# Attention's state products in 64x64 quarters of TensorE, and a mixture-of-experts opening taken by thirds of its tokens

## The chip, the cores and the metric

The kernel runs on one core of a Trainium2 chip. The metric is device time in microseconds (us) of one execution. All times compared here are of runs in the fast state (none is more than 1.5% above the fastest run of the same kernel); no slow run occurred. Beside the times, every run has a span (from its first to its last instruction) and a mean granted TensorE clock (1.00 is full speed), and each kernel has one profiled execution, from which all positions within the span are read. The span is 1.7 us or so shorter than the time of the same run.

## The reference

The program is a linear attention with a decaying state, then a mixture of eight experts with a balanced, greedy assignment. Everything is float32. Cut to what matters:

```python
B, H, S, D = 4, 8, 768, 48                   # r, k, v of this shape; decay w and bonus u per head and channel
for t in range(S):                           # attention
    kt, vt, rt = k[:, :, t], v[:, :, t], r[:, :, t]
    cur = einsum('bhd,bhe->bhde', u * kt, vt)
    y[:, :, t] = einsum('bhd,bhde->bhe', rt, state + cur)
    state = w[:, :, None] * state + einsum('bhd,bhe->bhde', kt, vt)
x = y.transpose(0, 2, 1, 3).reshape(3072, 384)
logits = x @ w_gate                          # 8 experts, 384 tokens each, taken in order of the logit
...
for e in range(8):
    mask = assigned == e
    out[mask] = relu(x[mask] @ w1[e]) @ w2[e]     # w1 384x1024, w2 1024x384
```

## The kernel before

Attention works in 24 units (4 batches x 6 chunks of 128 tokens; 8 heads, in 4 pairs). In each, TensorE transposes r and k, multiplies r with the state of the chunks before (`from_state`), forms the pair products inside the chunk (`pairs`), adds the outputs to the same bank of PSUM, the memory that holds TensorE's results (`outputs`) and forms the new state. The 8 heads' states lie in two row groups; every product from the state uses all 128 rows, half of which are zeros, and 64 columns:

```python
    y_pss, g_pss = ([ps.tile([128, HP, T], F32, ...) for i in range(2)] for name in "yg")   # two banks each
    def from_state(n):
        y_ps = y_pss[n % 2]
        if c > 0:
            for a in range(HP):
                for q in range(2):
                    nc.tensor.matmul(y_ps[halves[q], a, :], state[b][:, a, q, :], live[n]["rT"][:, a, :], start=(a == 0), ...)
    def outputs(n):
        ...                                                  # 8 products onto the same y_ps
        nc.scalar.copy(turned[n], y_ps)
        if c < C - 1:
            ...                                              # 8 products for the new state, kv_ps
            for q in range(2):
                nc.vector.tensor_add(own, own, kv_ps[heads[q]])      # 48 partitions
                nc.gpsimd.tensor_mul(own, own, wc)
    ...
            for n in range(N):                               # order on TensorE of one unit
                mild.rows_turned(n + 2); mild.keys_turned(n + 2); ...
                from_state(n)
                pairs(n + 1)
                outputs(n)
```

The experts come after that. For each expert a search on the logits, interleaved with the products of the expert before, yields a list of tokens; GpSimd fetches their rows from memory by an indirect transfer; TensorE transposes them (`turn`), multiplies with w1 (`hidden`, 8 columns of 128) and with w2 (`result`, 3 row groups of 8 products).

```python
    awake = ...
    for _ in range(7):                                       # keeps TensorE busy until the rows land
        nc.tensor.matmul(awake, ident, LG...)
    walk.settle(ahead, ask(number, w1), fetch(xg))           # rows by GpSimd, the whole of w1 by SyncE
    xT = turn(xg, ahead)
    for n in range(E):
        walk.behind = hidden(hid, 0, at["w1"], xT)
        ahead = following(...)                               # search for the next expert's tokens
        for j in range(1, KF):
            hidden(hid, j, at["w1"], xT)
        for c in range(NC):
            if c == NC - 1 and n + 1 < E:
                xT = turn(ahead["xg"])                       # next expert's transposes, one row group early
            result(n, c, hid, at["w2"], at["tok"])
```

## Time and profile before

The time before is 429.79 us (median of 3 runs, 428.57 to 432.33). The timeline of TensorE cuts the profiled span of 426.7 us into four parts. The first "list" is the small product that ends the search for the first expert's tokens, and the third part ends where the second expert's hidden products begin.

| part of the span, from TensorE's timeline | before, us |
|---|---|
| start to the first pair products | 13.91 |
| first pair products to the first list (140.06) | 126.15 |
| first list to the second expert's hidden products (187.86) | 47.80 |
| the rest | 238.84 |

The lines of attention, of VectorE beside it and of the gap before the first expert are in the prediction below. One stretch that it only tells is worth seeing, TensorE's timeline before around the second expert's list. The columns are start, duration, engine (PE is TensorE, DVE VectorE, ACT ScalarE, POOL GpSimd), line, operation, result and operands, shapes, number of records (a float32 product leaves two, a transpose one), and, in brackets, how long the engine idled before and what ended that.

```profile
170.88 0.18 PE L1133 MATMUL list_ps<-part,alike 128*128 128x12 f16 x1
170.92 10.95 PE L1267 MATMUL o_ps<-w,hid 128*128 128x384 f32 x32
181.71 0.82 PE L1249 MATMUL xT_ps<-ident,xg 128*128 128x128 f32 x6
```

Sixteen output products (32 records) lie between the list and the first transposes that need the listed rows. The rows land behind them, and there is no bracket: TensorE does not wait.

### The profile page before, as it was taken

The page shows a single profiled execution, that of the slowest core. Times are in us where ns is not written, and L with a number is a line of the kernel's source. Part 1 is how long each engine was busy: PE and PEld are TensorE (multiplying, and loading weights), DVE is VectorE, ACT ScalarE, POOL GpSimd, SP SyncE. Part 2 cuts the span into 40 slices and gives each one's busy share as a digit, 9 for nine tenths or more (in the row PEclk, how much of TensorE's full clock was granted, in tenths as well). Part 3 has the DMA queues.
Part 4 walks back from the last instruction along what each step waited for, and adds up shares of the span by engine and source line. Part 5 has one row for each costly group of instructions (what it writes and reads, how often), then busy time and mean ns, then how long its engine had stood idle before and what let it go on. Part 6 is the DMA issues. An engine that isn't in the chain of part 4 may idle for free. (4 is left out here: it accounts for less than half of the span.)

```text
span 426.7 us, 7898 instructions
## 1 busy us (share of the span) xinstructions
PE 405.7 (95%) x2926; PEld 271.6 (64%) x2926; DVE 206.6 (48%) x676; ACT 153.3 (36%) x390; POOL 122.0 (29%) x170
## 2 busy tenths in 40 slices
PE   6999999999998589999999999999999999999993
PEld 3788888888877345565565565565555555566551
DVE  5999889898758247218307506605703702000000
ACT  4888877777747022022122122122121211212200
POOL 5655866676300200310310310210130041211011
PEclk9999999999999699999999999999999999999999
DMA  9999999530018661910910830550460496201001
GB/s 145 170 174 183 168 185 154 116 73 2 3 57 313 205 231 47 324 38 7 336 47 18 260 129 21 193 197 18 152 238 18 144 325 217 75 18 37 2 18 37
DMA packets 93560, 54.38 MB, mean 127 GB/s; under 512 B 76736, under 2 KB 88128, under 8 KB 93504
## 3 DMA queue, kind: packets, MB, share of 16 engines
q1 hardware_dynamic: 89248, 42.49, 40.1%
q0 software_dynamic: 3072, 9.44, 6.2%
q10 hardware_dynamic: 1184, 1.77, 1.4%
q8 instruction: 27, 0.44, 0.5%
q14 instruction: 29, 0.24, 0.2%
HBM read 44.25 MB, written 9.44 MB: 126 GB/s over the span
## 5 line engine op out<-in xcount | busy, mean ns | idle before, releaser
L1260 PE MATMUL h_ps<-xT,w 128*128 128x384 f32 x384 | 133.3, 496 | 0.6 <-ACT xT L1250 0.6
L1267 PE MATMUL o_ps<-w,hid 128*128 128x384 f32 x384 | 129.4, 489 | 0.9
L1267 PEld LDWEIGHTS o_ps<-w,hid 128*128 128x128 f32 x384 | 71.1, 191 | 48.3 <-issue 4.4
L1260 PEld LDWEIGHTS h_ps<-xT,w 128*128 128x128 f32 x384 | 69.0, 191 | 41.8 <-issue 4.9
L1261 ACT ACTIVATE hid<-h_ps 128x384 f32<-128x384 f32 x64 | 31.4, 490 | 101.3 <-PE h_ps L1260 89.8
L1190 POOL DMA_INDIRECT xg<-x_rows,tok x24 | 23.5, 979 | 149.3 <-issue 106.7
L453 ACT ACTIVATE AT<-ident,dd 128x128 f32<-128x128 f32 x192 | 58.9, 394 | 2.0 <-DVE dd L448 2.0
L1270 POOL DMA_INDIRECT out_dram<-o_sb,tok x24 | 23.6, 982 | 113.9 <-ACT o_sb L1269 113.9
L1269 ACT COPY o_sb<-o_ps 128x384 f32<-128x384 f32 x24 | 11.5, 478 | 111.4 <-PE o_ps L1267 106.7
L847 DVE TENSOR_TENSOR own<-counts,same 128x64 f32<-128x64 f32 x21 | 4.7, 225 | 83.5 <-PE counts L859 83.5
L516 DVE COPY_PREDICATED AT<-mask,g_ps 128x512 f32<-128x512 uint8 x48 | 32.6, 732 | 8.6 <-PE g_ps L514 8.3
L514 PE MATMUL g_ps<-rT,kT 48*128 48x128 f32 x384 | 28.4, 285 | 0.2
L445 POOL TENSOR_TENSOR rk<-rk,u_bc 128x384 f32<-128x384 f32 x24 | 27.5, 1145 | 1.9
L444 POOL TENSOR_TENSOR rk<-rt,kt 128x384 f32<-128x384 f32 x24 | 24.2, 1007 | 9.3 <-DMA rt<-in_r_dram 4.4
L514 PEld LDWEIGHTS g_ps<-rT,kT 48*128 48x128 f32 x384 | 23.6, 187 | 4.3 <-issue 1.9
L535 PE MATMUL y_ps<-AT,vt 128*64 128x128 f32 x384 | 26.2, 279 | 0.0
L535 PEld LDWEIGHTS y_ps<-AT,vt 128*64 128x64 f32 x384 | 20.5, 137 | 2.8
L549 POOL TENSOR_TENSOR state<-state,wp 48x192 f32<-48x192 f32 x32 | 16.1, 502 | 20.5 <-DVE state L548 19.3
L524 PE MATMUL y_ps<-rT,state 128*64 128x128 f32 x320 | 21.8, 279 | 0.0
L434 DVE TENSOR_TENSOR ks<-kt,wk 128x384 f32<-128x384 f32 x24 | 20.4, 850 | 0.0
L524 PEld LDWEIGHTS y_ps<-rT,state 128*64 128x64 f32 x320 | 17.1, 137 | 3.1 <-issue 2.7
L473 ACT COPY kT<-kT_ps 128x512 f32<-128x512 f32 x24 | 14.0, 584 | 13.6 <-PE kT_ps L471 13.6
(189 smaller groups left out, 403.1 us busy)
## 6 DMA issues: line engine op xcount, KB each, us to landing
w<-in_moe_w_dram SPq DMA_DIRECT2D x15, 1536.0 KB, 8.3
kt<-in_k_dram SPq DMA_DIRECT2D x24, 192.0 KB, 4.2
rt<-in_r_dram SPq DMA_DIRECT2D x24, 192.0 KB, 4.2
vt<-in_v_dram SPq DMA_DIRECT2D x24, 192.0 KB, 4.9
x_rows<-AT SPq DMA_DIRECT2D x8, 192.0 KB, 2.7
w<-in_moe_w_dram ACTq DMA_DIRECT2D x1, 1536.0 KB
x_rows<-rt SPq DMA_DIRECT2D x6, 192.0 KB, 1.9
x_rows<-ks SPq DMA_DIRECT2D x5, 192.0 KB, 3.0
```

What stands on the lines that cost most here:

```text
L444: nc.gpsimd.tensor_mul(rk, rt[:, :, 0:D], kt)
L445: nc.gpsimd.tensor_mul(rk, rk, self.u_bc.rearrange("p (h d) -> p h d", h=H))
L453: self.tc.nc.scalar.activation(AT[:, h % 2, h // 2, :], self.ident, AF.Copy, scale=dd[:, h:h + 1])
L514: nc.tensor.matmul(g_pss[q][:, a, :], kT[heads[q], a, :], rT[heads[q], a, :], start=True, stop=True)
L516: nc.vector.copy_predicated(out=AT[:, q], mask=mask.unsqueeze(1).to_broadcast([128, HP, T]), data=g_pss[q])
L524: nc.tensor.matmul(y_ps[halves[q], a, :], state[b][:, a, q, :], live[n]["rT"][:, a, :], start=(a == 0), stop=False, skip_group_check=True)
L535: nc.tensor.matmul(y_ps[halves[q], a, :], vt[:, 2 * a + q, :], AT[:, q, a, :], start=(c == 0 and a == 0), stop=(a == HP - 1), skip_group_c ...
L1190: nc.gpsimd.indirect_dma_start(out=xg[:, c, :], out_offset=None, in_=x_dram, in_offset=bass.IndirectOffsetOnAxis(ap=tok[:, c:c + 1], axis=0))
L1260: product = nc.tensor.matmul(h_ps, w1[:, f, ts(j, 128)], xT[:, f, :], start=(f == 0), stop=(f == KD - 1))
L1261: nc.scalar.activation(hid[:, j, :], h_ps, AF.Relu)
L1267: nc.tensor.matmul(o_ps, hid[:, j, ts(c, 128)], w2[:, j, :], start=(j == 0), stop=(j == KF - 1))
L1270: nc.gpsimd.indirect_dma_start(out=out_rows[n * NC + c], out_offset=bass.IndirectOffsetOnAxis(ap=tok[:, c:c + 1], axis=0), in_=o_sb, in_of ...
```

## The change

It has two halves, which share no instruction.

*Attention.* The state is kept in four quarters, so that a product from it uses 48 rows and 64 columns and four such products are meant to lie side by side in the array. The rest follows from this: x gets one set of two PSUM banks instead of two sets of one, the next unit's pair products come ahead of the products from the state so that ScalarE has time to copy x out, both state additions become one over 128 partitions, and one product of 512 columns clears the state's bank at the start.

*First expert.* Half of w1 is asked for as soon as the expert is known, four filler products are to keep TensorE's clock up while the branch is left, and the first four of the eight columns of hidden products are opened by thirds: as soon as 128 of the 384 tokens are transposed, products with them begin.

```diff
+    y_ps = ps.tile([128, 2, HP, T], F32, name="y_ps")
+    order = [(g, j, i) for g in range(2) for j in range(2) for i in range(2)]
     def from_state(n):
         if c > 0:
+            for g, j, i in order:
+                a = 2 * g + i
+                nc.tensor.matmul(y_ps[halves[i], j, g, :], state[b][heads[j], a, :],
+                                 live[n]["rT"][heads[j], a, :], start=(g == 0), stop=False, skip_group_check=True)
-            for a in range(HP):
-                for q in range(2):
-                    nc.tensor.matmul(y_ps[halves[q], a, :], state[b][:, a, q, :], live[n]["rT"][:, a, :], ...
 ... (new_state: one addition and one scaling over 128 partitions)
+            nc.tensor.matmul(kv_ps, state[0][:, 0:2, :].rearrange("p a d -> p (a d)"),
+                             ident.unsqueeze(1).to_broadcast([128, HP, T]), start=True, stop=True)
 ... (the loop over units)
-                from_state(n)
                 if n + 1 < N:
                     pairs(n + 1)
+                from_state(n)
+                new_state(n)
                 outputs(n)
 ... (leaving the attention branch)
+        def between(most):
+            rows(most or N)
+            if not most:
+                for _ in range(4):
+                    nc.tensor.matmul(g_pss[0][:, 0:3, :], ident, ...)
 ... (first expert)
+        ask_half(ahead["fmax"])                       # half of w1, inside the branch
+    def opening(hid, at):
+        h_pss = [pool.tile([128, CAP], F32, name=name) for pool, name in ((ps_h, "h_ps"), (ps_o, "o_ps")) for _ in range(2)]
+        turn_rows(xT, at["xg"], 0)
+        for c in range(NC):
+            for j, h_ps in enumerate(h_pss):
+                product = products(h_ps, j, at["w1"], xT, ts(c, 128))
+                if j == 1 and c + 1 < NC:
+                    with tc.issue_after(product):
+                        copied = turn_rows(xT, at["xg"], c + 1)
+                    if c + 1 == NC - 2:
+                        with tc.issue_after(copied):
+                            weights(at["number"], at["w1"], slice(F // 2, F), nc.scalar)
+                            second(at, nc.scalar)
+        walk.behind = product
-    for _ in range(7):
+    for _ in range(4):
         nc.tensor.matmul(awake, ident, ...)
     for n in range(E):
+        if n == 0:
+            xT = opening(hid, at)
+            done = KF // 2
+        else:
             walk.behind = hidden(hid, 0, at["w1"], xT)
```

More of the change, by code (lines that the diff above doesn't have):

```diff
@@ L331, in __init__ @@
         nc.gpsimd.memset(self.wg_sb, 0.0)
-        for q in range(2):
-            nc.sync.dma_start(self.wg_sb[q * PD:q * PD + D, :, 0:E],
-                              wg.rearrange("(a q d) e -> q d a e", q=2, d=D)[q])
+        for i in range(2):
+            for j in range(2):
+                nc.sync.dma_start(self.wg_sb[i * PD:i * PD + D, j::2, 0:E],
+                                  wg.rearrange("(g i j d) e -> i j d g e", i=2, j=2, d=D)[i, j])
         self.load(3)
-        self.state = [const.tile([128, HP, 2, PD], F32, name=f"state{b}") for b in range(B)]
+        self.state = [const.tile([128, HP, PD], F32, name=f"state{b}") for b in range(B)]
         for t in self.state:
-            nc.scalar.activation(t.rearrange("p a q d -> p a (q d)"),
-                                 ident.unsqueeze(1).to_broadcast([128, HP, 128]), AF.Copy, scale=0.0)
+            nc.scalar.activation(t, ident[:, 0:PD].unsqueeze(1).to_broadcast([128, HP, PD]), AF.Copy, scale=0.0)
         mask = const.tile([128, 128], F32, name="mask_f")
@@ L396, in __init__ @@
             nc.vector.tensor_reduce(out=n_within, in_=n_ps, axis=AX.X, op=ALU.add)
-            flag = tab.tile([1, 1], I32, name="flag")
+            flag = const.tile([1, 1], I32, name="flag")
             nc.vector.tensor_single_scalar(out=flag, in_=n_within, scalar=float(H * PD), op=ALU.is_equal)
@@ L506, in attention_mild @@
     turned = [const.tile([128, HP, T], F32, name=f"xT{n}") for n in range(N)]
-    y_pss, g_pss = ([ps.tile([128, HP, T], F32, name=f"{name}_ps{i}") for i in range(2)] for name in "yg")
+    y_ps = ps.tile([128, 2, HP, T], F32, name="y_ps")
+    kv_ps = ps.tile([128, HP, T], F32, name="kv_ps")
+    g_pss = [ps.tile([128, HP, T], F32, name=f"g_ps{i}") for i in range(2)]
+    order = [(g, j, i) for g in range(2) for j in range(2) for i in range(2)]
     def pairs(n):
@@ L519, in from_state, with new_state @@
         b, c = units[n]
-        y_ps = y_pss[n % 2]
         if c > 0:
+            for g, j, i in order:
+                a = 2 * g + i
+                nc.tensor.matmul(y_ps[halves[i], j, g, :], state[b][heads[j], a, :],
+                                 live[n]["rT"][heads[j], a, :], start=(g == 0), stop=False, skip_group_check=True)
+    def new_state(n):
+        b, c = units[n]
+        vt, ks = (live[n][x] for x in ("vt", "ks"))
+        S0 = state[b]
+        if c < C - 1:
             for a in range(HP):
@@ L523, in from_state @@
                 for q in range(2):
-                    nc.tensor.matmul(y_ps[halves[q], a, :], state[b][:, a, q, :], live[n]["rT"][:, a, :],
-                                     start=(a == 0), stop=False, skip_group_check=True)
+                    nc.tensor.matmul(kv_ps[heads[q], a, 0:D], ks[:, 2 * a + q, 0:D], vt[:, 2 * a + q, 0:D],
+                                     start=True, stop=True)
+            own, new = S0[:, :, 0:D], kv_ps[:, :, 0:D]
+            wc = mild.w_chunk.unsqueeze(2).to_broadcast([128, HP, D])
@@ L527, in outputs @@
+            if c > 0:
+                nc.vector.tensor_add(own, own, new)
+                nc.gpsimd.tensor_mul(own, own, wc)
+            else:
+                nc.vector.tensor_mul(own, new, wc)
     def outputs(n):
         b, c = units[n]
-        vt, AT, ks = (live[n][x] for x in ("vt", "AT", "ks"))
-        y_ps = y_pss[n % 2]
-        S0 = state[b]
-        for a in range(HP):
-            for q in range(2):
-                nc.tensor.matmul(y_ps[halves[q], a, :], vt[:, 2 * a + q, :], AT[:, q, a, :],
-                                 start=(c == 0 and a == 0), stop=(a == HP - 1), skip_group_check=True)
@@ L537, in outputs @@
-        nc.scalar.copy(turned[n], y_ps)
-        if c < C - 1:
-            kv_ps = ps.tile([128, HP, D], F32, name="kv_ps")
-            for a in range(HP):
-                for q in range(2):
-                    nc.tensor.matmul(kv_ps[heads[q], a, :], ks[:, 2 * a + q, 0:D], vt[:, 2 * a + q, 0:D],
-                                     start=True, stop=True)
-            for q in range(2):
-                own = S0[heads[q], :, q, 0:D]
-                wc = mild.w_chunk[heads[q], :].unsqueeze(2).to_broadcast([D, HP, D])
-                if c > 0:
-                    nc.vector.tensor_add(own, own, kv_ps[heads[q]])
-                    nc.gpsimd.tensor_mul(own, own, wc)
-                else:
-                    nc.vector.tensor_mul(own, kv_ps[heads[q]], wc)
+        vt, AT = (live[n][x] for x in ("vt", "AT"))
@@ L553, in logits @@
+        for g, j, i in order:
+            a = 2 * g + i
+            nc.tensor.matmul(y_ps[halves[i], j, g, :], vt[:, 2 * a + j, :], AT[:, j, a, :],
+                             start=(c == 0 and g == 0), stop=(g == 1), skip_group_check=True)
+        nc.scalar.copy(turned[n].rearrange("p (g j) t -> p j g t", j=2), y_ps[:, :, 0:2, :])
     def logits(c):
@@ L575, in attention_mild @@
     spare += [t.rearrange("p h d -> p (h d)") for t in mild.vts]
+    banks = []
     def rows(most):
@@ L583, in rows @@
             b, c = units[n]
-            xr_ps = (y_pss + g_pss)[n % 4]
+            xr_ps = banks[n % len(banks)]
             for a in range(HP):
@@ L587, in rows @@
             xt = spare[n][:, 0:DX]
-            nc.scalar.copy(xt.rearrange("p (h d) -> p h d", h=H),
-                           xr_ps.rearrange("p a (q d) -> p (a q) d", q=2)[:, :, 0:D])
+            nc.scalar.copy(xt.rearrange("p (g i j d) -> p g j i d", i=2, j=2, d=D),
+                           xr_ps.rearrange("p (g j) (i d) -> p g j i d", j=2, i=2)[:, :, :, :, 0:D])
             nc.sync.dma_start(x_dram[ts(b * C + c, 128), :], xt)
@@ L608, in attention_mild @@
                 if n + 2 < N:
-                    mild.diagonal(n + 2)
-                from_state(n)
-                if n > B and n % B == 1:
-                    by_token(n // B - 1)
+                    mild.diagonal(n + 2, 0, 4)
                 if n + 1 < N:
                     pairs(n + 1)
+                if n > 0 and n % B == 0:
+                    logits(n // B - 1)
+                if n + 2 < N:
+                    mild.diagonal(n + 2, 4)
+                from_state(n)
+                new_state(n)
+                if n > 0 and n % B == 0:
+                    by_token(n // B - 1)
                 outputs(n)
@@ L617, in attention_mild @@
                     mild.own(n + 3)
-                if n > 0 and n % B == 0:
-                    logits(n // B - 1)
                 if n == N - 3:
@@ L631, in attention_mild @@
                 pass
+            banks += g_pss + [y_ps[:, 0], kv_ps]
             rows(1)
@@ L636, in attention_mild @@
         tags = {"counts": "kT_ps", "few": "rT_ps"}
+        def between(most):
+            rows(most or N)
+            if not most:
+                for _ in range(4):
+                    nc.tensor.matmul(g_pss[0][:, 0:3, :], ident, ident.unsqueeze(1).to_broadcast([128, 3, 128]),
+                                     start=True, stop=True)
         first(arm=ctx, bank=lambda shape, name, tag: mild.ps.tile(shape, F32, name=name, tag=tags[tag]),
-              between=lambda most: rows(most or N))
+              between=between)
 class Assignment:
@@ L887, in search, with settle @@
         self.tokens(out["place"], out["tok"])
-    def settle(self, out, ask, fetch):
+    def settle(self, out, ask, fetch, asked=False):
         fetch(out["tok"])
-        ask(out["fmax"])
+        if not asked:
+            ask(out["fmax"])
         found = self.nc.values_load(out["flag"][0:1, 0:1], min_val=0, max_val=1,
@@ L1132, in tokens @@
         list_ps = self.bank([128, NC, Q], "list_ps", "few")
-        nc.tensor.matmul(list_ps.rearrange("p c q -> p (c q)"), self.alike, part, start=True, stop=True)
-        self.between(0)
+        listed = nc.tensor.matmul(list_ps.rearrange("p c q -> p (c q)"), self.alike, part, start=True, stop=True)
+        with self.tc.issue_after(listed.ins):
+            self.between(0)
         mine = pool.tile([128, NC, Q], F32, name="mine")
@@ L1173, in rwkv5_eagle_then_base_layer_balanced, with ask @@
     walk = Assignment(ctx, tc, LG, CAP)
-    def ask(number, w1):
+    def ask(number, w1, cols=slice(0, F)):
         def by(fmax):
@@ L1179, in by, with weights @@
                                     op0=ALU.mult, op1=ALU.add)
-            nc.sync.dma_start(w1, moe_w1[which(number, nc.sync)].rearrange("o (c p) f -> p (o c) f", p=128))
+            weights(number, w1, cols, nc.sync)
         return by
+    def weights(number, w1, cols, queue):
+        queue.dma_start(w1[:, :, cols], moe_w1[which(number, queue)].rearrange("o (c p) f -> p (o c) f", p=128)[:, :, cols])
     def which(number, queue):
@@ L1200, in rwkv5_eagle_then_base_layer_balanced @@
     ahead = dict(walk.slots(), number=number, w1=w1, xg=xg)
+    ask_half = ask(number, w1, slice(0, F // 2))
     def first(arm, bank, between=walk.between):
@@ L1242, in following, with turn_rows, turn @@
         return at
-    def turn(xg, late=None):
+    def turn_rows(xT, xg, c):
+        xT_ps = ps_t.tile([128, KD, 128], F32, name="xT_ps")
+        for f in range(KD):
+            nc.tensor.transpose(xT_ps[:, f, :], xg[:, c, ts(f, 128)], ident)
+        return nc.scalar.copy(xT[:, :, ts(c, 128)], xT_ps).ins
+    def turn(xg):
         xT = xpool.tile([128, KD, CAP], F32, name="xT")
         for c in range(NC):
-            xT_ps = ps_t.tile([128, KD, 128], F32, name="xT_ps")
-            for f in range(KD):
-                nc.tensor.transpose(xT_ps[:, f, :], xg[:, c, ts(f, 128)], ident)
-            copied = nc.scalar.copy(xT[:, :, ts(c, 128)], xT_ps)
-            if c == 0 and late:
-                with tc.issue_after(copied.ins):
-                    second(late, nc.scalar)
-        return xT
+            turn_rows(xT, xg, c)
+        return xT
@@ L1257, in hidden, with products @@
+    def products(h_ps, j, w1, xT, cols=slice(0, CAP)):
+        for f in range(KD):
+            product = nc.tensor.matmul(h_ps[:, cols], w1[:, f, ts(j, 128)], xT[:, f, cols],
+                                       start=(f == 0), stop=(f == KD - 1))
+        return product.ins
     def hidden(hid, j, w1, xT):
         h_ps = ps_h.tile([128, CAP], F32, name="h_ps")
-        for f in range(KD):
-            product = nc.tensor.matmul(h_ps, w1[:, f, ts(j, 128)], xT[:, f, :], start=(f == 0), stop=(f == KD - 1))
+        product = products(h_ps, j, w1, xT)
@@ L1261, in hidden @@
         nc.scalar.activation(hid[:, j, :], h_ps, AF.Relu)
-        return product.ins
+        return product
+    def opening(hid, at):
+        xT = xpool.tile([128, KD, CAP], F32, name="xT")
+        h_pss = [pool.tile([128, CAP], F32, name=name) for pool, name in ((ps_h, "h_ps"), (ps_o, "o_ps")) for _ in range(2)]
[11 more added lines that the diff above has]
+        walk.behind = product
+        for j, h_ps in enumerate(h_pss):
+            nc.scalar.activation(hid[:, j, :], h_ps, AF.Relu)
+        return xT
@@ L1272, in result @@
             in_=o_sb, in_offset=None)
-    awake = ps_o.tile([128, DX], F32, name="o_ps")
-    for _ in range(7):
-        nc.tensor.matmul(awake, ident, LG.rearrange("p i e -> p (i e)")[:, 0:1].to_broadcast([128, DX]),
-                         start=True, stop=True)
-    walk.settle(ahead, ask(number, w1), fetch(xg))
-    xT = turn(xg, ahead)
+    awake = ps_t.tile([128, KD, 128], F32, name="xT_ps")
+    for _ in range(4):
+        nc.tensor.matmul(awake, ident, ident.unsqueeze(1).to_broadcast([128, KD, 128]), start=True, stop=True)
+    walk.settle(ahead, ask_half, fetch(xg), asked=True)
     for n in range(E):
@@ L1283, in rwkv5_eagle_then_base_layer_balanced @@
         hid = hpool.tile([128, KF, CAP], F32, name="hid")
-        walk.behind = hidden(hid, 0, at["w1"], xT)
+        done = 1
+        if n == 0:
+            xT = opening(hid, at)
+            done = KF // 2
+        else:
+            walk.behind = hidden(hid, 0, at["w1"], xT)
         if n + 1 < E:
             ahead = following(n + 2 == E)
-        for j in range(1, KF):
+        for j in range(done, KF):
             hidden(hid, j, at["w1"], xT)
```

## The prediction

> **What bounds the kernel now.** I read the page's slices first, then the timeline of one attention unit, then the stretch between attention and the first expert. The slices (40 of 10.67 us each):
>
> ```profile
> PE   6999999999998589999999999999999999999993
> ...
> PEclk9999999999999699999999999999999999999999
> DMA  9999999530018661910910830550460496201001
> ```
>
> TensorE is at 9 almost everywhere; only the start and slices 12 to 14 (about 128 to 149 us) have holes, and slice 13 is also the only one with a lower granted clock. DMA is high to about 75 us, but loads run ahead: 24 units of 590 KB at some 175 GB/s are 3.4 us per unit, less than a unit takes. The timeline of TensorE in one such unit (start, duration, what):
>
> ```profile
> 98.62 0.66 PE L460 MATMUL rT_ps<-ident,rt 128*128 128x128 f32 x4
> 99.11 0.60 PE L471 MATMUL kT_ps<-ident,ks 128*128 128x128 f32 x4
> 99.64 1.09 PE L524 MATMUL y_ps<-rT,state 128*64 128x128 f32 x16
> 100.67 1.16 PE L514 MATMUL g_ps<-rT,kT 48*128 48x128 f32 x16
> 101.76 1.09 PE L535 MATMUL y_ps<-AT,vt 128*64 128x128 f32 x16
> 102.68 0.53 PE L542 MATMUL kv_ps<-vt,ks 128*48 128x48 f32 x16
> ```
>
> From start to start: 0.49, 0.53, 1.03, 1.09, 0.92 and 0.46 (the next unit begins at 103.14), together 4.52 us with no hole. So TensorE sets the pace. VectorE is close behind it:
>
> ```profile
> 99.50 0.55 DVE L448 TENSOR_REDUCE dd<-rk 128x8 f32<-128x384 f32 x1
> ...
> 100.09 0.69 DVE L465 TENSOR_TENSOR rT<-rT_ps,wr 128x512 f32<-128x512 f32 x1
> ...
> 100.48 1.00 POOL L444 TENSOR_TENSOR rk<-rt,kt 128x384 f32<-128x384 f32 x1
> ...
> 100.70 1.20 DVE L434 TENSOR_TENSOR ks<-kt,wk 128x384 f32<-128x384 f32 x1
> ...
> 101.93 1.36 DVE L516 COPY_PREDICATED AT<-mask,g_ps 128x512 f32<-128x512 uint8 x2
> ...
> 103.26 0.74 DVE L548 TENSOR_TENSOR state<-state,kv_ps 48x192 f32<-48x192 f32 x2
> ```
>
> That is 4.54 us of VectorE rows per 4.52 us (neighbours overlap a little), 1.20 of it a product that elsewhere takes 0.67: it ended 0.42 us after GpSimd's product beside it ended. The third place is the gap before the first expert:
>
> ```profile
> 140.48 0.17 DVE L1140 TENSOR_REDUCE tok<-mine 128x3 int32<-128x12 f32 x1
> 143.43 0.14 DVE L1178 TENSOR_SCALAR number<-fmax 1x1 int32<-1x1 f32 x1 [2.78 <-issue]
> ...
> 144.08 6.83 PE L1277 MATMUL o_ps<-LG,ident 128*128 128x384 f32 x14 [3.84 <-issue]
> ...
> 152.39 1.05 PE L1249 MATMUL xT_ps<-ident,xg 128*128 128x128 f32 x6 [0.66 <-DMA xg<-x_rows,tok]
> ...
> 154.06 2.17 PE L1260 MATMUL h_ps<-xT,w 128*128 128x384 f32 x6 [0.61 <-ACT xT L1250]
> ```
>
> The token list is ready at 140.65, but the first expert product starts at 154.06: 2.8 us leaving the branch, seven wake-up products at half clock (the windows show a granted 0.50 from 142 to 148 us), and token rows that take 6.0 to 6.6 us to land because the 1.5 MB of w1 is issued among them. From then on TensorE is full: hidden products to 170.92, output products to 187.86.
>
> **What the Trainium skill says.** "TensorEngine Tiling (Array Packing)", Tiling Modes: in 64x64 mode there are 4 independent tiles, and changing the mode drains TensorE. The trace agrees with such overlap for the modes used: half-array products go at 0.92/16 = 57 ns a record, and the logits in 4 column tiles at 1.01/32 = 32 ns. No trace of before shows 64x64 tiles. "TensorE: Matmul & The Clock Gate", Wait — 56ns, not 53.3ns?: starts never lie closer than about 25 ns; the 48-wide products here go at 0.46/16 = 29 ns. Same page, What's actually happening: an idle window of about 3.4 us halves the clock; the trace has that 0.50. "SBUF — State Buffer", Who interferes with whom: a VectorE operation with two SBUF inputs and a GpSimd read exclude each other, as the 1.20 us product shows.
>
> **The change, part by part.**
>
> *Products from the state in quarters.* The same 8 products (16 records), but each uses 48 rows and 64 columns, so four can run side by side instead of two. Ideal: half of 0.92 = 0.46 us; at 29 to 32 ns a record, 0.46 to 0.51. I keep the mode-change cost, as the number of changes in a unit stays four. Saving 0.46 us in the 20 units that have an earlier state: **-9.2 us**. The new unit is 4.06 us.
>
> *Does another engine take over?* VectorE: the state's two additions of 192 columns (0.37 each) become one across 128 partitions, and GpSimd's two scalings likewise: VectorE -0.37, GpSimd -0.5. After the addition GpSimd needs 0.1 + 0.54 + 1.0 us before the ks product is free to run 0.4 more, VectorE then 1.36 of masks and 0.37 of addition: about 3.9 us round, also with 0.45 us of the search's constants between. ScalarE: 0.58 + 0.58 + 2.45 = 3.61 us. Both fit under 4.06, by 0.15 and 0.4, so small waits are possible.
>
> *x in one set of two banks.* It is single-buffered now: products from the state (or the unit's first output products) wait for ScalarE's copy of the previous unit. Two banks let the row halves write different banks. With transposes and pair products put ahead there are about 2.1 us between, and the copy needs 0.2 + 0.58: hidden in the steady state. It is not hidden in the first units, where ScalarE is late (before: its first x copy started only at 22.54 after 2.07 us idle), nor in the last unit, which has no transposes and no pair products ahead (0.75, partly under the search's 0.4 us product): +0.1 and **+0.3 us**.
>
> *A product of 512 columns into the state bank at the start*, to set its contents: two records of 512 columns, at the 325 ns that 384 columns take, **+0.85 us** on TensorE just before the first pair products at 13.90, where TensorE soon is the pace. By my hand schedule the first units lose what units 4 and 5 gain.
>
> Attention in sum: -9.2 + 0.85 + 0.1 + 0.3 = **-8.0 us**.
>
> *First expert.* The order of instructions shows half of w1 asked for inside the branch, after the row writes (about 140 us), so its 0.77 MB is over before the token rows are asked for; four filler products (2.6 us at full clock) cover 140.2 to 142.9, so the clock should stay. Token rows asked for at 143.5, 145.0 and 146.2 then need nearer the 3.1 us minimum in the trace: there from about 146.8. Four wake-up products end near 146.7, transposes start at 147.0, first products at 148.0. Thirds: 36 products of 128 columns, 72 records; the late transposes give 0.66/6 = 110 ns a record, so 7.9 us, hardly more than 12 x 0.65 = 7.8. With the two later sets of transposes the opening ends at about 156.6, where before the same four columns of hidden products would end near 162.
>
> *What is given back.* The second expert's search now starts after the whole opening (156.6), and by the order its list comes 21 products (13.7 us) and 0.7 us of search products later, at 171.0: no earlier than before (170.88). But only 7 output products (4.6 us) follow it before TensorE asks for the transposes of its rows; before there were 16. In the trace the rows land 7.8 and some 9.0 us after the list. So TensorE waits about 4 us here. End of the first expert: 171.0 + 9.0 + 0.33 + 0.65 + 0.33 + 7 x 0.65 = 185.9 against 187.86: **-2.0 us**, not the 6 that the opening alone gains.
>
> Sum: -10.0 us. I give back 1 us for small waits of VectorE and the longer branch exit if instruction loads meet w1's transfer: 429.8 - 9.0 = **420.8 us**.
>
> **The rivals.**
> 1. *Quarters don't overlap fourfold*: if each matmul's two records keep TensorE as long as a half did, the 9.2 us vanish, and with the 0.85 us product and the single buffer the attention gets about 1 us slower; total near 428. Against it: the logits' 32 ns in four column tiles.
> 2. *VectorE becomes the pace*: with its product held by GpSimd longer, the unit goes to some 4.3 us and attention gains 3 to 4 us; total near 425. For it: the slack is only 0.15 us.
> 3. *No wait at the second expert*, if its rows land 3 us sooner: 3 us better, near 417.5. Against: the 5.9 to 6.6 us landings there.
>
> **Range and chances.** Rival 1 I give one in ten, rival 2 two in ten, rival 3 one in six. 2% is 8.6 us, thus 421.2, almost my centre: 8 in 10 within 416.5 to 425.5, faster 0.53, within 2% 0.45, slower 0.02.
>
> **What would show it.** Quarters: the state products' group from start to start near 0.55 to 0.6 us and units 4.0 to 4.1 us apart; holes before it, released by ScalarE's x copy or by VectorE, would speak for the rivals. Clock: no 0.5 between 142 and 148 us less the shift. Opening: token rows landing in 3 to 4 us, the opening's end about 5 us earlier relative to the token list. Give-back: about 4 us of idle TensorE before the second expert's transposes, ended by the row transfer. I am wrong if the units stay above 4.3 us, if the branch exit grows beyond 4 us, or if that wait is missing.

## The result, and the profile after

The changed kernel is correct. It takes 425.25 us (median of 4 runs, 424.38 to 425.36), against 429.81 us of 4 runs of the kernel before. A ratio is always the mean time of one kernel's fast runs over that of the kernel before in the same rounds, so it is not quite the ratio of the medians; here it is 0.9882, with a 95% interval of 0.9836 to 0.9928. That is within 2%. The mean clock of the core was 0.987 to 0.990 in the four runs.

| part of the span | before | after | difference | predicted |
|---|---|---|---|---|
| start to the first pair products | 13.91 | 15.20 | +1.29 | +0.85 |
| first pair products to the first list | 126.15 | 118.24 | -7.91 | -8.8 |
| first list to the second expert's hidden products | 47.80 | 51.30 | +3.50 | -2.0 |
| the rest | 238.84 | 238.86 | 0.0 | 0 |
| span | 426.7 | 423.6 | -3.1 | |

The predicted column holds the prediction's own terms; its further +1.0 us was a reserve for small waits of VectorE and a longer branch exit. TensorE's timeline of one attention unit after the change:

```profile
93.81 0.66 PE L460 MATMUL rT_ps<-ident,rt 128*128 128x128 f32 x4
...
95.93 0.67 PE L529 MATMUL y_ps<-rT,state 48*64 48x128 f32 x16
96.53 0.56 PE L539 MATMUL kv_ps<-vt,ks 128*48 128x48 f32 x16
96.92 1.06 PE L555 MATMUL y_ps<-AT,vt 128*64 128x128 f32 x16
97.91 0.55 PE L460 MATMUL rT_ps<-ident,rt 128*128 128x128 f32 x3
```

The products from the state, 48 rows by 64 columns now, go from start to start in 0.60 us instead of 1.03, and the unit in 97.91 - 93.81 = 4.10 us instead of 4.52. No line has a bracket: nothing makes TensorE wait. VectorE in the same unit does wait for TensorE, so it has not become the pace:

```profile
94.51 0.69 DVE L465 TENSOR_TENSOR rT<-rT_ps,wr 128x512 f32<-128x512 f32 x1 [0.46 <-PE rT_ps L460]
...
96.10 1.36 DVE L522 COPY_PREDICATED AT<-mask,g_ps 128x512 f32<-128x512 uint8 x2 [0.43 <-PE g_ps L520]
```

The first expert is where the time was lost. TensorE's timeline after, from the first list on:

```profile
133.44 0.18 PE L1158 MATMUL list_ps<-part,alike 128*128 128x12 f16 x1 [0.57 <-DVE part L1156]
...
137.03 2.82 PE L1333 MATMUL xT_ps<-ident 128*128 128x384 f32 x8 [0.73 <-PE g_ps L658]
140.79 0.55 PE L1278 MATMUL xT_ps<-ident,xg 128*128 128x128 f32 x3 [0.94 <-DMA xg<-x_rows,tok]
142.02 2.57 PE L1289 MATMUL h_ps<-xT,w 128*128 128x128 f32 x12 [0.69 <-DVE low L952]
...
146.77 1.50 PE L1289 MATMUL h_ps<-xT,w 128*128 128x128 f32 x12
...
152.46 0.25 PE L883 MATMUL counts<-prop,ind 128*128 128x64 bf16 x3
...
167.27 0.18 PE L1158 MATMUL list_ps<-part,alike 128*128 128x12 f16 x1
167.31 4.76 PE L1323 MATMUL o_ps<-w,hid 128*128 128x384 f32 x14
176.73 0.87 PE L1278 MATMUL xT_ps<-ident,xg 128*128 128x128 f32 x3 [4.67 <-DMA xg<-x_rows,tok]
```

Three things are to be seen. First, the hidden products begin at 142.02, 8.6 us after the list (before: 14.0 us, by the prediction's line at 154.06). Second, twelve narrow records take 2.57 us at 142.02 and 1.50 us at 146.77: the same work at two clocks. Third, after the second list there are only seven output products (14 records), and then TensorE stands for 4.67 us until the second expert's rows have landed, and 0.21 us more; the transposes after that are slow again (0.87 us for three here and 0.90 for the next three; before, six took 0.82). The clock by stretches of 2 us (columns: stretch, time and busy time of TensorE with its number of records, granted clock, share of the DMA engines, GB/s) puts both together:

```profile
142.00:144.00 2.00, 1.98 (x11) 0.61 0.00 0
144.00:146.00 2.00, 2.00 (x12) 0.54 0.00 0
...
176.00:178.00 2.00, 1.05 (x4) 0.64 0.68 248
178.00:180.00 2.00, 2.00 (x6) 0.50 0.08 29
```

GpSimd's timeline shows that at this second list a store of finished output rows, at 167.92, was issued ahead of the first fetch of rows, at 169.22. The first fetch thus comes 1.95 us after the list, where before it came 1.41 us after it (172.29 - 170.88). From the first fetch's issue to the transposes is 176.73 - 169.22 = 7.5 us.

### The profile page after: what moved, and what is told of

Same layout as the page of the kernel before. It is cut to its first block, busy times and chain, and to the rows that moved or that the text cites. A ratio compares the mean times of both kernels' runs of the same rounds, so it can differ in the third digit from the quotient of the medians.

```text
span 423.6 us, 7986 instructions
## 1 busy us (share of the span) xinstructions
PE 401.4 (95%) x2978; PEld 266.5 (63%) x2978; DVE 198.4 (47%) x656; ACT 153.6 (36%) x390; POOL 113.4 (27%) x154
## 5 line engine op out<-in xcount | busy, mean ns | idle before, releaser
L1289 PE MATMUL h_ps<-xT,w 128*128 128x384 f32 (+1 forms) x396 | 130.5, 479 | 0.7 <-DVE low L952 0.7
L1296 ACT ACTIVATE hid<-h_ps 128x384 f32<-128x384 f32 x60 | 29.5, 492 | 94.0 <-PE h_ps L1289 84.2
L1279 ACT COPY xT<-xT_ps 128x384 f32<-128x384 f32 x24 | 11.0, 485 | 24.1 <-PE xT_ps L1278 14.8
L434 DVE TENSOR_TENSOR ks<-kt,wk 128x384 f32<-128x384 f32 x24 | 19.4, 808 | 0.0
L465 DVE TENSOR_TENSOR rT<-rT_ps,wr 128x512 f32<-128x512 f32 x24 | 16.4, 684 | 5.3 <-PE rT_ps L460 5.2
L1278 PE MATMUL xT_ps<-ident,xg 128*128 128x128 f32 x72 | 12.1, 294 | 5.8 <-DMA xg<-x_rows,tok 5.8
## 6 DMA issues: line engine op xcount, KB each, us to landing
w<-in_moe_w_dram SPq DMA_DIRECT2D x14, 1536.0 KB, 10.5
```

The source lines that it names most:

```text
L434: self.tc.nc.vector.tensor_mul(self.live[n]["ks"][:, :, 0:D], self.live[n]["kt"], self.wk.rearrange("p (h d) -> p h d", h=H))
L1289: product = nc.tensor.matmul(h_ps[:, cols], w1[:, f, ts(j, 128)], xT[:, f, cols], start=(f == 0), stop=(f == KD - 1))
L1296: nc.scalar.activation(hid[:, j, :], h_ps, AF.Relu)
```

## The experiments

Theory: attention gains what it promised, the opening by thirds itself gains too, and the loss lies in the second expert, whose rows now have seven output products to hide behind instead of sixteen, together with the half clock after each wait. Rivals: the two halves disturb each other; the narrow products themselves cost the time; the clock in the opening does; the store ahead of the fetch does. Each kernel was timed in 5 rounds against the kernel before; all are correct and all runs fast. Three batches of four were run; in them the kernel before had medians of 428.35, 429.13 and 428.94 us. The second batch (two columns by thirds, seven awake, and the two runs of attention's order) ran on another chip, so kernels of different batches are compared by their ratios. In the table, "first expert" is the profiled time from the first list to the second expert's hidden products (47.8 before, 51.3 after).

| run | median us | ratio to before (95%) | first expert, us |
|---|---|---|---|
| attention half only | 422.14 | 0.9843 (0.9809 to 0.9877) | 47.8 |
| first-expert half only | 431.81 | 1.0081 (1.0049 to 1.0112) | 49.5 |
| six wake-up products | 425.28 | 0.9909 (0.9876 to 0.9941) | 52.4 |
| whole opening | 420.38 | 0.9816 (0.9782 to 0.9850) | 46.6 |
| two columns by thirds | 418.35 | 0.9748 (0.9721 to 0.9775) | 46.0 |
| whole opening, seven awake | 421.36 | 0.9821 (0.9794 to 0.9847) | 47.7 |
| new order with halves | 428.45 | 0.9981 (0.9964 to 0.9998) | not used |
| quarters in the old order | 423.66 | 0.9883 (0.9851 to 0.9914) | not used |
| transposes last | 418.75 | 0.9759 (0.9737 to 0.9780) | 44.9 |
| two columns, six awake | 418.87 | 0.9770 (0.9747 to 0.9794) | 45.5 |
| two columns, memset start | 418.09 | 0.9732 (0.9708 to 0.9756) | 45.5 |
| one column by thirds | 418.92 | 0.9770 (0.9744 to 0.9796) | 45.1 |

### The two halves alone

The edits are the two halves of the diff. The first kernel has the attention half only:

> The attention half of the change alone (quarters, new order, x in one set of two banks, the 512-column product); the first expert as in the kernel before. Theory A (the attention gains 6.6 us, as its token list came at 133.4 instead of 140.1 us, and the first expert loses some 3.5 us of it): 6.6 us faster than before, near 423 us, and faster than the whole change by about 2 us. Theory B (the attention's gain lets something later wait longer, whatever the first expert does): near the whole change's 425 us.

The second has the first-expert half only:

> The first expert's half of the change alone (half of w1 early, filler products, thirds of tokens), with the attention as before. Theory A: 3 to 4 us slower than before, near 433 us, with a wait of 4 to 5 us before the second expert's transposes and a granted clock near 0.5 while the opening products begin. Theory B: the same as before or faster.

Measured: attention alone is 1.6% faster than before, and its first expert takes 47.8 us as before. (That it beats the whole change is not resolved: the intervals of 0.9843 and 0.9882 overlap.) The first-expert half alone is 0.8% or 3.5 us slower, with waits of 4.27 and 0.43 us at its second expert, though its opening had the full clock in the profile; this profile is of the fastest of its seven runs, so that its 49.5 us understate the loss. The two changes add up to a ratio of 0.992, inside the interval of the whole change. So the halves do not disturb each other by more than the noise, and the second half of the change loses time by itself.

### The wait at the second expert: transposes last, whole opening

The most direct test leaves the opening as it is and takes the cause of the wait away: the second expert's transposes are issued behind all output products of the first.

```diff
-            if c == NC - 1 and n + 1 < E:
+            if c == NC - 1 and 0 < n and n + 1 < E:
                 xT = turn(ahead["xg"])
             result(n, c, hid, at["w2"], at["tok"])
+        if n == 0:
+            xT = turn(ahead["xg"])
```

> The changed kernel with one edit: the second expert's transposes are issued after all of the first expert's output products instead of in the midst of them, so that some 10 more output products lie between the second list and the wait for its rows. Theory (the wait of 4.7 + 0.2 us of TensorE for the rows of the second expert is what the change made in the first expert, together with the slow clock that follows it): the wait is under 0.5 us, from the list to the end of the first expert's output products is some 47 us instead of 51.3, and the time is about 420.5 us, 1.0 to 1.5 per cent under the changed kernel (some of the gain is lost because the copies after the transposes are no longer hidden: some 1.2 us). Rival (the rows' landing is not what the time hangs on; only the place of the idle time moves): 424 to 426 us.

TensorE's timeline of this run at the second list:

```profile
164.84 0.18 PE L1158 MATMUL list_ps<-part,alike 128*128 128x12 f16 x1
...
169.79 5.40 PE L1323 MATMUL o_ps<-w,hid 128*128 128x384 f32 x16
175.02 0.82 PE L1278 MATMUL xT_ps<-ident,xg 128*128 128x128 f32 x6
176.14 0.55 PE L1278 MATMUL xT_ps<-ident,xg 128*128 128x128 f32 x3 [0.29 <-ACT xT L1279]
177.25 2.20 PE L1289 MATMUL h_ps<-xT,w 128*128 128x384 f32 x6 [0.57 <-ACT xT L1279]
```

Fifteen output products (30 records) lie behind the list instead of seven, and the wait for the rows is gone; what is left, 0.29 and 0.57 us, is for ScalarE's copies, which no longer lie beside products. From the second list to the second expert's products is 177.25 - 164.84 = 12.4 us instead of 17.5. The ratio went from 0.9882 to 0.9759, 1.2 points or some 5 us, about what this stretch gained. The theory holds: this wait, with the slow clock behind it, is the loss. GpSimd's store is ahead of the first fetch here too (165.49 and 166.79) and yet no wait for rows is left: this order put the fetch off by some 0.5 us, but it does not decide. In the profile the first expert gained 1.3 us more, because its opening ran at the full clock; how far that holds for the runs without a profile, and so whether the opening has a part in the 5 us, is not shown (below).

The other direction gives up the thirds: the first expert transposes all rows and then opens as before, but keeps the early half of w1.

```diff
+    def whole(at):
+        for c in range(NC):
+            copied = turn_rows(xT, at["xg"], c)
+            if c == 1:
+                with tc.issue_after(copied):
+                    weights(at["number"], at["w1"], slice(F // 2, F), nc.scalar)
+                    second(at, nc.scalar)
...
-            xT = opening(hid, at)
-            done = KF // 2
-        else:
-            walk.behind = hidden(hid, 0, at["w1"], xT)
+            xT = whole(at)
+        walk.behind = hidden(hid, 0, at["w1"], xT)
```

> The whole change, but the first expert opens with all its tokens at once as before; half of w1 early and the filler are kept. Theory A: the second expert's list comes ahead of the output products again, 16 of these lie between it and the transposes, and the wait of 4.7 us goes; the first expert ends some 5 us sooner than in the whole change: near 420 us, also 3 us less than the attention half alone because rows land sooner. Rival: if the thirds gain what they were meant to gain, this is slower than the whole change (above 425).

It met its expectation: no wait at the second expert, a first expert of 46.6 us, 420.38 us (but only 1.8 us less than the attention half alone, not 3). That the narrow products themselves are dear is not the reason: at full clock 12 narrow records went from start to start in 1.35 us (the run with the transposes last), so the 18 of one column take 2.0 us, and six records of 384 columns take 1.99. Its opening ran at clocks of 0.55 and 0.60 from 144 to 148 us, so it is not the best place to stop either.

### How much by thirds

Two columns instead of four:

```diff
-        h_pss = [pool.tile(...) for pool, name in ((ps_h, "h_ps"), (ps_o, "o_ps")) for _ in range(2)]
+        h_pss = [pool.tile(...) for pool, name in ((ps_h, "h_ps"),) for _ in range(2)]
...
-                if j == 1 and c + 1 < NC:
+                if j == 0 and c + 1 < NC:
...
-            done = KF // 2
+            done = KF // 4
```

> The whole change, but only two of the eight hidden columns are made by thirds before the second expert's search starts. Theory A (what costs is that the search's start, and with it the landing of the second expert's rows, is put off): the opening is half as long, 13 output products instead of 7 come between the list and the transposes, so the wait of 4.9 us falls to about 1 us and the total to 421 to 422 us. Rival (the wait comes from the transfers alone, wherever the list comes): the wait stays near 4 to 5 us and the total near 425.

It did better than expected. TensorE's timeline at its second list:

```profile
163.85 0.18 PE L1158 MATMUL list_ps<-part,alike 128*128 128x12 f16 x1
163.89 9.02 PE L1323 MATMUL o_ps<-w,hid 128*128 128x384 f32 x26
...
173.74 0.52 PE L1278 MATMUL xT_ps<-ident,xg 128*128 128x128 f32 x3 [0.51 <-DMA xg<-x_rows,tok]
```

The search for the second expert starts when the opening is over. Here that is 15.4 us after the first list instead of 19.0; the second list comes 30.2 us after the first instead of 33.8, with thirteen output products behind it instead of seven, and the wait shrinks to 0.51 us. In this kernel GpSimd issues the row fetches ahead of the output store. Against the whole opening (0.9748 and 0.9816, intervals apart) some opening by thirds gains; part of that may be the clock, whose mean is 0.987 to 0.991 in the five runs there and 0.996 to 0.998 in six of seven here.

One column (the edit is a single tile in the list and `done = 1`):

> The changed kernel with the opening by thirds for one of the eight columns only (the two-column version has the best time so far). Theory: one column by thirds gives the rows' transposes too little work between them to hide the second and third third's landing and copies, but one h product more lies after the second list; from the list to the end of the first expert's outputs 46 to 47 us against 46.0 with two columns, the wait at the second expert under 0.5 us, time 418 to 420 us. Rival (fewer columns by thirds is always better, as the narrow products cost more): 417 us.

No wait at the second expert, as the theory had it; but TensorE now pauses 0.57 and 0.58 us inside the opening for copies. The first expert takes 45.1 us, the time is 418.92 us, and the intervals of one and two columns overlap: the choice between them is open.

### The clock in the opening: wake-up products

The changed kernel with six instead of four wake-up products:

> The whole change with six wake-up products instead of four, so that TensorE works until the first token rows land. Theory A1 (the half clock of the opening is due to the pause after the wake-up products, 139.9 to 142.0 us): clock 1.0 in the opening, which then takes some 2 us less; total 1.5 to 2 us less than the whole change, near 423.5. Rival A2 (opening is bound by the landing of rows, the clock doesn't matter): no change in time, the first product starts no sooner and the third set of rows is waited for.

This missed, and the rival's unchanged time came in. The opening had the full clock and ended 18.1 us after the list instead of 19.0, but the waits at the second expert were 3.70 and 1.94 us, the clock behind them 0.5, and the time 425.28 us: a sooner opening does not help while the rows of the next expert set the end.

The whole opening with seven:

> As the whole-opening run, with seven wake-up products instead of four, which last until about the landing of the first rows. Theory: the clock stays at 1.0 through the opening, where the first product of the whole-opening run took 3.6 instead of 2.2 us; 1 to 1.5 us less than that run, 419 us or a little more. Rival: the rows' landing sets the start, and a late pause lets the clock fall all the same: no difference (420.4).

This missed as well, again as the rival had it: 0.9821 against 0.9816. The products waited 1.55 us for ScalarE's copy (ScalarE also issues the weights' transfers between the copies); the clock fell all the same, to 0.50 and 0.69 from 146 to 150 us.

The two-column kernel with six:

> The kernel with two columns of the opening by thirds, with 6 instead of 4 wake-up products ahead of the first rows. Theory: the granted clock of the opening, 0.50 to 0.89 at 142 to 148 us, becomes 1.0 and, since here no long wait follows at the second expert (0.5 us before), most of it is kept: 0.5 to 1.5 us less, about 417.3 us. Rival: the added products delay the rows' transposes or the gain goes into a longer wait at the second expert, as it did where all columns go by thirds: 418 to 419 us.

The profile shows the clock of 1.0 that was expected, but no gain: 418.87 us, the rival's figure. The list of single runs says why. The profiled run of the two-column kernel with four wake-up products had a mean clock of 0.993 and took 420.16 us; its other six runs had 0.996 to 0.998 and took 417.86 to 418.71 us. The slow stretch that I meant to remove was there in one run of seven, the profiled one.

So the instructions alone do not decide whether the clock falls in the opening. The kernel with the transposes last has the same instructions up to there as the changed kernel; the changed kernel's profile shows 0.61 and 0.54, the other's 1.00. Between the end of the wake-up products and the first hidden products TensorE worked 0.55 us of 142.02 - 139.85 = 2.17 us in the one and 0.55 of 141.23 - 139.13 = 2.10 us in the other. "TensorE: Matmul & The Clock Gate", What's actually happening, says that the window in which activity is judged is free-running and about 3.4 us long, so that the point of change differs from run to run. The traces agree in the length: from 142 to 146 us the changed kernel lacks 0.39 and 0.46 of 2 us each, together 1.70 us, which at half clock is a stretch of 3.4 us; from 176 to 180 us it lacks 1.72 us, once more such a stretch; the kernel before lacks 3.42 us from 140 to 150 us, twice as much. Where the windows lie in a run is not shown.

The mean clock tells what the runs without a profile lack. For the profiled run of the changed kernel 0.990 over 423.6 us is 4.2 us, and its windows lack 4.0 us: 1.70, 1.72 and 0.6 at the very end. Its three other runs (0.987 and 0.988) lack 5.1 to 5.5 us, hence as much or more, while the five with the transposes last lack 0.8 to 2.1 us (1.2 in the profile, all of it at the end). So the slow clock of the changed kernel is no accident of its profiled run. Whether its other runs lack the time in the opening or behind the wait, where the run with six wake-up products lost two such stretches (3.4 us from 174 to 184 us), stays open.

### Attention: order and quarters

Only the new order, in the kernel before, with its half products:

```diff
-    def outputs(n):            # products for the new state move into new_state(n)
+    def new_state(n):
...
+                    pairs(n + 1)
...
                 from_state(n)
+                new_state(n)
                 outputs(n)
```

> The kernel before with nothing but the new order of the attention's products (pair products first, state update before the outputs); halves, two sets of banks, first expert as before. Theory A (the attention's gain is the quarters' alone): units stay 4.5 us apart, time equal to before within 1 us, 428 us. Rival (the order itself removes waits): several us faster, units near 4.1 us.

TensorE's timeline of the second half of one unit of it:

```profile
99.78 1.09 PE L524 MATMUL y_ps<-rT,state 128*64 128x128 f32 x16
...
101.06 1.06 PE L554 MATMUL y_ps<-AT,vt 128*64 128x128 f32 x16
102.05 0.66 PE L460 MATMUL rT_ps<-ident,rt 128*128 128x128 f32 x4
```

The next group, the new-state products, begins at 100.71, so the products from the state go from start to start in 0.93 us instead of 1.03, and the unit takes 4.39 us instead of 4.52, though each product is the same. In time that is little, as expected: 0.2%, with 124.53 instead of 126.15 us from the first pair products to the list in the profile. The other way round, quarters in the old order (the edit is shown against the attention half alone):

```diff
-                    pairs(n + 1)        # ahead of from_state
                 from_state(n)
-                new_state(n)
+                    pairs(n + 1)
                 outputs(n)
+                new_state(n)
```

> The attention half alone with the old order: products from the state ahead of the pair products, one set of two banks for x. Theory A: only the 1.5 us of state update and transposes lie between the outputs and the next products from the state, which still covers the copy's 0.75 us, so units stay at 4.1 us and the total equals the attention half alone (422 us) within 1 us. Rival (the new order is needed because of the single set of banks): waits for the copy before each product from the state, units of 4.3 us or more, total 425 or more.

Here the unit takes 4.10 us, as in the changed kernel; only two of the last units have waits (0.78 and 0.38 us, for ScalarE's copy). The units met the expectation; the time is 0.9883 against 0.9843 for the attention half alone, 1.7 us more and not within the 1 us expected, with intervals that overlap. So quarters save 0.42 us per unit whichever the order. The new order saves 0.13 us per unit with halves and nothing with quarters; a likely reason is that in the new order the half products, the new-state products and the outputs, all of 128 rows and at most 64 columns, follow each other without a change of tile shape, where the pair products lay between them before. Quarters have a shape of their own and are rid of no change. "TensorEngine Tiling (Array Packing)", Tiling Modes, says that TensorE drains at a change; the runs show the 0.13 us, not the drain. With quarters, its use is at the end: from the first pair products to the list, 118.36 us in the attention half alone against 118.65 us in the old order.

### The start product

The two-column kernel with the 512-column product replaced:

```diff
-            nc.tensor.matmul(kv_ps, state[0][:, 0:2, :].rearrange("p a d -> p (a d)"),
-                             ident.unsqueeze(1).to_broadcast([128, HP, T]), start=True, stop=True)
+            nc.vector.memset(kv_ps, 0.0)
```

> The kernel with two columns of the opening by thirds, with the new start product of the attention (one 128x512 product of 1.05 us that clears both banks of the state) replaced by a VectorE memset of the bank. Theory (this product lies on the path to the first unit, and its share of the time is what the prediction said, 0.85 us): the first unit's pair products start at 13.9 to 14.4 us instead of 15.2, and the time is 0.5 to 1.0 us less. Rival (it lies beside the wait for the first rows and costs nothing, or the memset of VectorE stands in front of work that the first unit needs): the same time within 0.3 us, or more.

(The expectation's "both banks" is the one bank of 512 columns.) TensorE's timeline of the start, first of the changed kernel:

```profile
14.15 1.12 PE L604 MATMUL kv_ps<-ident,state 128*128 128x512 f32 x2
15.20 1.16 PE L520 MATMUL g_ps<-rT,kT 48*128 48x128 f32 x16
```

and then of this run:

```profile
13.38 0.66 PE L471 MATMUL kT_ps<-ident,ks 128*128 128x128 f32 x4 [0.68 <-ACT kT L473]
14.12 1.16 PE L520 MATMUL g_ps<-rT,kT 48*128 48x128 f32 x16
```

In the changed kernel the second key transposes began at 13.37. From there to the first pair products is 1.83 us with the product and 0.74 without: it costs 1.09 us on the path, where 0.85 had been predicted. The moment itself is a poor measure, because it differs from run to run by more than that: with the product it was 14.12 us in the run with the transposes last and 15.36 in the two-column run, according to how long TensorE still ran slowly before: the two records of 384 columns at 7.5 us took 0.81 us in the first, those at 7.7 us 1.49 us in the second. From the first pair products to the list, however, every profile of quarters in the new order has 118.23 to 118.44 us. In time the memset is not resolved: 0.9732 against 0.9748, overlapping intervals. In the profile its wait at the second expert was 1.78 us instead of 0.51, because the fetch landed 8.3 us after its issue (in the two-column run some 7.2, 173.74 - 166.55); why is open. It has the lowest ratio of the study, 418.09 us or 2.7% under the kernel before, and is faster than the changed kernel; from the other kernels with one or two columns by thirds and from the transposes last it is not resolved.

## Why the prediction was right or wrong

The measured 425.25 us is inside the range of 416.5 to 425.5, but 0.25 us from its upper end and 4.5 us above the centre. "Faster" had 0.53 and "within 2%" 0.45; it is within 2%. That the number is inside is in part luck: one term of the sum had the wrong sign and was off by 5.5 us.

- **TensorE is the bound in attention, and quarters run faster: right.** Rivals 1 and 2 are refuted by the unit of 4.10 us without a bracket and by VectorE's waits for TensorE.
- **-9.2 us for the quarters: right in kind, a little too large.** It took half of 0.92 us off and kept the cost of a change of shape, so that the state products were to go from start to start in 1.03 - 0.46 = 0.57 us ("near 0.55 to 0.6"). They take 0.60 us, and the unit saves 0.42 instead of 0.46. Over 20 units that is 0.8 us, nearly all of the difference between -8.8 and -7.91.
- **+0.85 us for the start product: right in kind, too small**, 1.09 us by the memset. The wait for the last unit's copy of x, predicted as +0.3, is 0.36 us.
- **-2.0 us for the first expert: wrong, and the step that failed.** It measured +3.5. The prediction put the opening's end 16.5 us behind the list, the second list 14.4 us behind that and the second expert's products 14.9 us behind that one. Measured: 19.0, 14.8 and 17.5, thus +2.5, +0.4 and +2.6 us.
  - The first +2.5: the products began 8.6 us behind the list instead of 7.9 (148.0 - 140.06), +0.6 us, as the first rows landed 4.1 us after they were asked for, not near 3.1; and "so the clock should stay" did not hold in the profiled run. From the first product to the opening's end it took 10.44 us, where the kernel with the transposes last, at full clock, took 8.79 and the prediction 8.6. So the clock's share is 1.65 us, and 0.2 us remain.
  - The last +2.6 has two parts. The transposes of the second set of rows began 10.5 us behind the list (177.81) instead of 9.0, +1.5 us: the first fetch was issued 0.5 us later behind the list than before, by the store ahead of it, and the second took 7.2 us to land. From there to the second expert's products it took 6.93 instead of 0.33 + 0.65 + 0.33 + 7 x 0.65 = 5.86 us, +1.1 us: the half clock after the wait, which the prediction did not have; from 176 to 180 us the windows show 0.64 and 0.50.
- **"TensorE waits about 4 us here": right** (4.67 + 0.21 us), and rival 3 refuted. The mechanism was seen beforehand, only the sum was drawn too kindly: a wait long enough to lose the clock costs more than its length.
- **"No 0.5 between 142 and 148 us less the shift": not borne out** in the profiled run; the same instructions kept the full clock in the profile with the transposes last.
- **Rows landing in 3 to 4 us: right**, 4.1 and 3.2 us for two of the three fetches, 6.0 and 6.6 before. **The opening's end about 5 us earlier: too large.** It is 19.0 us behind the list, where the prediction's own figure for before is 162 - 140.06 = 21.9: 2.9 us, and 4.3 us in the run at full clock (17.7).
- **The reserve of 1 us** was not needed where it was meant: VectorE makes TensorE wait nowhere in attention, and from the list to the first fetch of rows it is 3.16 us (136.60 - 133.44) instead of 3.42, so that the branch exit did not grow.
- **"Exclude each other, as the 1.20 us product shows": half shown.** That product overlapped GpSimd's for 0.78 us (100.70 to 101.48) and took 0.53 us longer than 0.67. The line shows a delay, not a full exclusion.

What remains open is how much of the 0.60 us the change of shape takes, and what sets the clock in the opening of a single run.

## What to carry to other kernels

When a stretch is made shorter at its beginning, ask what the next stage's data will then hide behind: here the opening by thirds moved work ahead of the search, so that seven instead of sixteen products were left behind the list, and moving the nine transposes to the end recovered some 5 us. A long wait of TensorE is to be counted with the slow clock that may follow it (here it followed waits of 4.67, 4.27 and 3.70 us, and not one of 1.78 us). And before a clock dip in a profile is repaired, look at the mean clock of the other runs: the dip may belong to that one execution (two columns by thirds) or to all of them (the changed kernel).

## What the Trainium skill lacked or had wrong

- "TensorEngine Tiling (Array Packing)", Tiling Modes, names four independent 64x64 tiles and a drain at a change of mode, without a duration for either; the speed-ups that the pages give as measured are for tiles of 32 rows or columns and 512 columns. Here eight float32 products in 64x64 tiles took 0.60 us where they took 1.03 us (0.93 us in the other order) in 128x64 tiles: 1.7 or 1.55 times, not twice. The order of the same products was worth 0.13 us per unit.
- "TensorE: Matmul & The Clock Gate", What's actually happening, gives an idle window of about 3.4 us for the half clock. Here the clock was halved after 2.17 us in which TensorE still worked 0.55 us and which had no idle time longer than 0.94 us; another run of the same instructions (0.55 of 2.10 us) kept the full clock, and an idle time of 1.78 us amid dense work kept it as well (the kernel with the memset: fourteen records of output products behind it in 4.68 us, as elsewhere at full clock).
- "DMA: Bandwidth & Descriptors", Anatomy of one DMA — SWDGE (gpsimd) path, has a fixed cost of about 2.0 us per transfer and a rate, by which I estimate 2.5 us for 128 rows of 1.5 KB. The indirect fetches of such rows landed in 2.9 us at the least, in a median of 6.2 us and in 7.2 us at the most in the changed kernel (8.3 us in the kernel with the memset); no page has a figure for an indirect fetch beside a load of weights.
